# Turning query and key images by DMA instead of TensorE in a four-layer recurrent attention kernel

## The chip, the cores and the metric

One core of one Trainium2 chip. The metric is the device time of one execution in microseconds (us), as the median of several executions.

Names in the profile: PE is TensorE (matrix products), DVE and ACT are the engines that in this kernel copy out of PSUM and do elementwise work, SP is the queue that issues its DMAs. The granted clock is the share of TensorE's full clock that the chip allowed. The chain is the path of work that ended last, followed back from the last instruction. A DMA's landing is the time from its issue to its data's arrival; its hold is the time that its instruction occupies the issuing queue.

## The reference, cut to what matters

```python
def _A_ref(x, mem0, Wq, Wk, Wv, Wo, seg_len):      # "memory layer"; 64 segments of 32 tokens
    mem = mem0                                      # 8 memory tokens
    for s in range(n_seg):
        h = concat([mem, x[:, s*32:(s+1)*32]])      # 40 tokens
        q, k, v = h @ Wq, h @ Wk, h @ Wv            # 32 heads of 128
        p = softmax(where(mask, q @ k.T * scale, -1e9))
        o = (p @ v) @ Wo
        mem = o[:, :8]                              # goes into the next segment
        outs.append(o[:, 8:])
    ...
x = x + _A_ref(layernorm(x), ...)                   # memory layer
x = x + _B_ref(layernorm(x), ...)                   # linear attention layer
x = x + _A_ref(layernorm(x), ...)
x = x + _B_ref(layernorm(x), ...)
```

The memory layers are a recurrence: a segment can't start until the memory of the one before is there. They take 1893 of 2158 us before.

## The kernel before

The kernel lists operations as nodes with reads, writes and an estimated cost. A list scheduler in the kernel's own code turns them into one fixed order for each engine, so what runs when is decided by those estimates.

A segment's 32 tokens are split: the first 24 form a block of 32 columns with the 8 memory tokens, and the last 8 tokens of four segments form a "left block" per tile of 128 tokens. Projections put four heads side by side in the four 32-column strips of TensorE, so that an "image" (128 x 512) has tokens in its partitions. The kernel's score products read queries and keys with the head dimension in the partitions. So each image is evacuated from PSUM, transposed by four 128x128 products on TensorE, and evacuated again:

```python
def transposed(W, key, blk, bkeys, b, dst, dkey, urgent):
    tl = project(W, key, blk, bkeys, b, urgent)     # 16 products of 512 columns, mode "col"
    k = img_no[0] % NI
    img_no[0] += 1
    nd = evac(img[:, k, :], lambda: tl.f32()[:, :], 512, tiles=[tl], writes=[("img", k)], urgent=urgent)
    tt = P.tile()
    def tr(pe):
        for i in range(4):
            r = pe.transpose(tt.bf16()[:, 128 * i:128 * i + 128], img[:, k, 128 * i:128 * i + 128], id_sb[:, :])
        return r
    add("pe", tr, c_pe(4, 128), reads=[("img", k), "id"], tiles=[tt], urgent=urgent)
    evac(dst, ..., 512, tiles=[tt], writes=[dkey], rate=2, urgent=urgent)
    return nd
```

A segment needs four images: query and key of heads 0 to 15 (b = 0), then of heads 16 to 31 (b = 1). A left block needs four more for each tile. The mask enters the memory scores as a bias product of 16 rows, twice 128 columns. Token scores are one product for each head and strip, over a query buffer into which the 8 left columns are copied.

The softmax here doesn't subtract the row's maximum and nothing guards it: scores larger than these inputs give would overflow.

Of the kernel before, what the change touches and what calls it, by code (L numbers as in the profile page):

```python
# [18 lines left out]
MODE_SLACK = 0.3  # L19
# [35 lines left out]
class _Node:  # L55
    __slots__ = ("engs", "fn", "cost", "sync", "order", "tiles", "dsem", "dval", "eng", "start", "done",
                 "tail", "sig", "val", "waits", "know", "idx", "succ", "nleft", "urgent", "mode")


class _Prog:  # L60
# [17 lines left out]
    def add(self, engs, fn, cost, reads=(), writes=(), tiles=(), dsem=None, urgent=False, mode="full",  # L78
            after=()):
        nd = _Node()  # L80
        nd.mode = mode
        nd.engs = (engs,) if isinstance(engs, str) else tuple(engs)
# [41 lines left out]
    def schedule(self):  # L124
# [15 lines left out]
        for nd in reversed(nodes):  # L140
            lag = PE_LAG if nd.engs == ("pe",) else HOP
            best = 0.0
            for s in nd.succ:
                v = s.tail + (0.0 if nd in s.order else lag)
                if v > best:
                    best = v
            nd.tail = best + min(nd.cost.values())
# [13 lines left out]
        n_left = len(nodes)  # L161
        pend = {e: [] for e in ENGINES}
# [25 lines left out]
        def n_free(t_now):  # L188
            k = 0
            for own in self.bank_owner:  # L190
                if own is None or (own.ops[-1].done is not None and own.ops[-1].done <= t_now):
                    k += 1
            return k
# [3 lines left out]
        def pick_for(e):  # L197
            tn = self.now[e]
            while pend[e] and pend[e][0][0] <= tn + EPS:
                _, _, nd = heapq.heappop(pend[e])  # L200
                if nd.done is None:
                    heapq.heappush(ready[e], (-nd.tail, nd.idx, nd))
            pick = None
            kept = []
            while ready[e]:
# [4 lines left out]
                if first_of(nd):  # L210
                    bf = bank_for(tn)
                    if bf is None or bf[1] > tn + EPS or (not nd.urgent and n_free(tn) < 3):
# [12 lines left out]
                elif nd.tail < pick.tail - MODE_SLACK:  # L225
# [12 lines left out]
        while n_left:  # L238
# [47 lines left out]
            nd.done = nd.start + nd.cost[e]  # L286
            self.now[e] = nd.done - (0.09 if e == "act" else 0.05 if e == "dve" else 0.0)
# [94 lines left out]
def _build_kernel(nc, A_x, A_mem0, A_Wq, A_Wk, A_Wv, A_Wo, A_seg_len, B_wqkv, B_wo, out):  # L382
# [35 lines left out]
    w16_sb = sb("w16_sb", [128, 4, 2, 32])  # L418
# [31 lines left out]
    img = av(NI * 512).rearrange("p (r x) -> p r x", r=NI)  # L450
    vimg = av(2 * 1024).rearrange("p (r x) -> p r x", r=2)
    vleft = av(2 * 1024).rearrange("p (r x) -> p r x", r=2)
    qT = av(2 * 1280).rearrange("p (r h j x) -> p r h j x", r=2, h=8, j=4)
# [11 lines left out]
    xlnA = av(D).rearrange("p (r x) -> p r x", r=1)  # L465

# [73 lines left out]

    BIG = -1.0e9
    pool(lambda g: g.memset(w16_sb[:, :, 0, :], 0.0), ["w16"])
    pool(lambda g: g.memset(w16_sb[:, :, 1, :], BIG), ["w16"])
    for gg in range(4):
        a = w16_sb[:, gg, 0, :]
        sel(a, GE, BIG, 0, [[-4, 4], [0, 8]], 1, "w16")
        sel(a, GE, BIG, 3, [[4, 4], [0, 8]], -1, "w16")
        sel(w16_sb[:, gg, 1, :], ALU.not_equal, 0.0, -gg, [[-4, 4], [0, 8]], 1, "w16")
# [71 lines left out]
    def a_layer(layer):  # L620
        img_no = [0]
# [14 lines left out]
        def transposed(W, key, blk, bkeys, b, dst, dkey, urgent):  # L636

            tl = project(W, key, blk, bkeys, b, urgent)
            k = img_no[0] % NI
            img_no[0] += 1  # L640
            nd = evac(img[:, k, :], lambda: tl.f32()[:, :], 512, tiles=[tl], writes=[("img", k)], urgent=urgent)
            tt = P.tile()

            def tr(pe):
                for i in range(4):
                    r = pe.transpose(tt.bf16()[:, 128 * i:128 * i + 128], img[:, k, 128 * i:128 * i + 128], id_sb[:, :])  # L646
                return r
            add("pe", tr, c_pe(4, 128), reads=[("img", k), "id"], tiles=[tt], urgent=urgent)
            evac(dst, lambda: tt.bf16()[:, 0:512].rearrange("p (h j x) -> p h j x", h=4, j=4), 512, tiles=[tt],
                 writes=[dkey], rate=2, urgent=urgent)  # L650
            return nd

        def left_block(G):
# [3 lines left out]
            for b in range(2):  # L657
                hs = slice(4 * b, 4 * b + 4)
                transposed(Wq_sb, "Wq", blk, bk, b, qTl[:, r2, hs, :, :], ("qTl", r2, b), False)
                transposed(Wk_sb, "Wk", blk, bk, b, kTl[:, r2, hs, :, :], ("kTl", r2, b), False)  # L660
# [29 lines left out]
        def mem_attention(s, b, early):  # L690
# [8 lines left out]
            def bias(pe):  # L699
                for a in range(2):  # L700
                    r = pe.matmul(tl.f32()[:, 128 * a:128 * a + 128], u16_sb[0:16, :],  # L701
                                  w16_sb[0:16, g, a, :].unsqueeze(1).to_broadcast([16, 4, 32]), start=(a == 0),
                                  stop=False, skip_group_check=True)
                return r
            add("pe", bias, c_pe(2, 128), reads=["u16", "w16"], tiles=[tl], urgent=True, after=early, mode="bias")
# [38 lines left out]
        def x_attention(s):  # L744
# [6 lines left out]
            for b in range(2):  # L751
                hs = slice(4 * b, 4 * b + 4)
                add(ANY, copy(qT[:, r2, hs, :, 32:40], qTl[:, g2, hs, :, gl]),
                    {"act": c_act(128, 0, 1), "dve": c_dve(128)}, reads=[("qTl", g2, b)], writes=[("qTL", r2, b)])

                def mm(pe, b=b):
                    for hh in range(4 * b, 4 * b + 4):
                        for j in range(4):
                            r = pe.matmul(tl.f32()[32 * j:32 * j + 32, 32 * hh:32 * hh + 32], kT[:, r2, hh, j, :],  # L759
                                          qT[:, r2, hh, j, 8:40], start=True, stop=True, tile_position=(0, 32 * j))  # L760
                    return r
                add("pe", mm, c_pe4(16, 32), reads=[("kT", r2, b), ("qT", r2, b), ("qTL", r2, b)], tiles=[tl], mode="col")
# [58 lines left out]
        def next_mem(s):  # L821
            G1, g1 = divmod(s + 1, 4)
            tl = P.tile()
            for h in range(2):
# [5 lines left out]
                add("pe", mm, c_pe(2, 128), reads=[(("outW", s % 3), h), "selm"], tiles=[tl], urgent=True)  # L830
# [5 lines left out]
        def residual(G, g):  # L836

            if g == 0:
# [5 lines left out]
                c_pe(1, 512), reads=[(("outW", w), 0), (("outW", w), 1), "selx"], tiles=[tl])  # L844
            if g == 3:
# [3 lines left out]
                    c_pe(1, 512), reads=[("outWl", 0), ("outWl", 1), "sell"], tiles=[tl])  # L849
                add("dve", lambda v: v.tensor_tensor(x_sb[:, G, :], x_sb[:, G, :], tl.f32()[:, :], ALU.add), c_dve(512),  # L850
                    reads=[("x", G)], writes=[("x", G)], tiles=[tl])

# [192 lines left out]
```

## Time and profile before

| | before |
|---|---|
| time, median of 3 runs | 2161.87 us (2161.3 to 2163.71) |
| TensorE busy | 2079 us, 96% of the span |
| DVE, ACT busy | 1201 us, 1160 us |
| granted TensorE clock | 0.994 |
| TensorE in the chain that ended last | 94% |

The prediction below shows the lines behind this table and how its numbers come from them. Some durations that it uses, as medians of this trace: products overlap (four of 512 columns start 0.216 us after the four before and last 0.38 us each); the reader of a product's result in PSUM starts 0.21 to 0.30 us after the start of the last product, for products of 32 and 128 columns at L710, L646 and L759; a copy of 512 columns from PSUM takes DVE 0.42 us where PSUM holds bf16 (the transposed images) and 0.69 us where it holds f32 (0.52 and 1.04 ns for each further column, by the 96- and 128-column copies at 0.21 and 0.29 us), and ACT 0.60 us in both cases.

### The profile page before, as it was taken

The numbers are of one execution on the slowest core, as the hardware profiler recorded it, in microseconds if no ns is written. First come the engines' busy times: TensorE is split into PE (matmuls) and PEld (weight loads), VectorE is DVE, ScalarE is ACT, GpSimd is POOL, SyncE is SP. The second block draws the span as 40 slices with busy tenths as digits, with TensorE's granted clock in tenths as the row PEclk, the third lists the DMA queues.
The fourth block names the chain that finished last, engine by engine and source line by source line (L and its number), as shares of the span: only waits on it lengthen the run. The fifth ranks groups of instructions, "written<-read, shape, count | busy, mean of one in ns | idle before, by whom it ended". The sixth has DMA issues, their size and how long they took to land.

```text
span 2158.2 us, 83024 instructions
## 1 busy us (share of the span) xinstructions
PE 2079.3 (96%) x37982; PEld 1163.5 (54%) x37982; DVE 1201.2 (56%) x3287; ACT 1159.7 (54%) x3112; POOL 14.8 (1%) x74
## 2 busy tenths in 40 slices
PE   1999999999999999998999999999999999999989
PEld 0555555555555555554655555555555555555545
DVE  0655555555554555556876555555555555554678
ACT  0555555555555555554645555555555555555554
POOL 2000000000000000000000000000000000000000
PEclk9999999999999999999999999999999999999999
DMA  9000000000000000001000000000000000000011
GB/s 350 3 3 2 3 3 3 3 3 3 3 3 3 3 3 3 3 3 41 1 2 3 3 3 3 3 2 3 3 3 3 3 3 3 3 3 3 3 41 40
DMA packets 12558, 30.48 MB, mean 14 GB/s; under 512 B 424, under 2 KB 9648, under 8 KB 10672
## 3 DMA queue, kind: packets, MB, share of 16 engines
q1 hardware_dynamic: 12208, 25.18, 3.2%
q8 instruction: 297, 4.87, 0.9%
q14 instruction: 53, 0.43, 0.1%
HBM read 23.08 MB, written 2.10 MB: 12 GB/s over the span
## 4 chain that ended last, share of the span: by engine, by line
PE 94%; DVE 2%; DMA 2%; ACT 1%; issue 0%; SPq 0%
PE pb L630 42%; PE pb L808 14%; PE pb L646 8%; PE pb L792 4%; PE pb L827 3%; PE pb L921 3%; PE pb L710 3%; PE pb L701 3%; PE pb L842 2%; PE pb L722 2%; DMA x_sb<-in_A_x_dram 2%; PE pb L735 2%; PE pb L759 2%; PE pb L914 1%; PE pb L736 1%; PE pb L771 1%
## 5 line engine op out<-in xcount | busy, mean ns | idle before, releaser
L498 ACT ACTIVATE arena_sb<-pb 128x512 bf16<-128x512 f32 (+6 forms) x1410 | 673.2, 492 | 458.7 <-PE pb L630 269.7
L630 PE MATMUL pb<-Wq_sb,arena_sb 128*32 128x512 bf16 x5120 | 478.2, 383 | 0.9 <-ACT arena_sb L498 0.4
L630 PE MATMUL pb<-Wk_sb,arena_sb 128*32 128x512 bf16 x5120 | 472.5, 382 | 0.0
L499 DVE CAST arena_sb<-pb 128x512 bf16<-128x512 f32 (+2 forms) x541 | 312.3, 578 | 237.6 <-PE pb L793 142.5
L630 PE MATMUL pb<-Wv_sb,arena_sb 128*32 128x512 bf16 x5120 | 374.4, 383 | 0.0
L808 PE MATMUL pb<-Wo_sb,arena_sb 128*32 128x512 bf16 x5184 | 350.1, 381 | 0.0
L780 DVE TENSOR_TENSOR arena_sb<-arena_sb 32x256 bf16<-32x256 bf16 x512 | 213.3, 417 | 133.6 <-ACT arena_sb L776 121.7
L499 DVE COPY arena_sb<-pb 128x512 bf16<-128x512 bf16 (+1 forms) x543 | 205.8, 399 | 137.8 <-PE pb L646 134.3
L646 PE MATMUL pb<-id_sb,arena_sb 128*128 128x128 bf16 x2560 | 216.7, 220 | 0.0
L630 PEld LDWEIGHTS pb<-Wq_sb,arena_sb 128*32 128x32 bf16 x5120 | 134.4, 96 | 133.2 <-ACT arena_sb L498 14.6
L646 PEld LDWEIGHTS pb<-id_sb,arena_sb 128*128 128x128 bf16 x2560 | 145.0, 97 | 103.2 <-issue 41.6
L630 PEld LDWEIGHTS pb<-Wk_sb,arena_sb 128*32 128x32 bf16 x5120 | 134.6, 97 | 108.5 <-issue 2.5
L717 ACT ACTIVATE arena_sb<-pb 128x256 bf16<-128x256 f32 x256 | 97.5, 381 | 158.9 <-PE pb L710 158.8
L498 ACT ACTIVATE outW_sb<-pb 128x256 fp32r<-128x256 f32 x198 | 75.8, 383 | 195.9 <-PE pb L808 194.5
L808 PEld LDWEIGHTS pb<-Wo_sb,arena_sb 128*32 128x32 bf16 x5184 | 119.7, 95 | 102.4 <-issue 20.7
L630 PEld LDWEIGHTS pb<-Wv_sb,arena_sb 128*32 128x32 bf16 x5120 | 109.6, 95 | 76.9
L782 DVE TENSOR_TENSOR arena_sb<-arena_sb 32x64 bf16<-32x64 bf16 x512 | 111.0, 217 | 15.8
L792 PE MATMUL pb<-arena_sb 128*128 128x128 bf16 x1024 | 115.2, 218 | 4.0 <-DVE arena_sb L782 4.0
L710 PE MATMUL pb<-arena_sb 128*128 128x32 bf16 x2048 | 118.6, 177 | 0.0
L499 DVE COPY arena_sb<-arena_sb 128x128 bf16<-128x128 bf16 x192 | 35.9, 194 | 128.8 <-PE pb L759 127.8
L793 PE MATMUL pb<-arena_sb 128*128 128x32 bf16 x1024 | 105.6, 178 | 0.0
L827 PEld LDWEIGHTS pb<-selm_sb,outW_sb 128*128 128x128 f32 x504 | 77.6, 188 | 51.8 <-ACT outW_sb L498 18.2
(108 smaller groups left out, 2330.6 us busy)
## 6 DMA issues: line engine op xcount, KB each, us to landing
Wq_sb<-in_A_Wq_dram SPq DMA_DIRECT2D x1, 4096.0 KB, 12.4
Wk_sb<-in_A_Wk_dram SPq DMA_DIRECT2D x1, 4096.0 KB, 22.2
Wv_sb<-in_A_Wv_dram SPq DMA_DIRECT2D x1, 4096.0 KB, 31.7
Wo_sb<-in_A_Wo_dram SPq DMA_DIRECT2D x1, 4096.0 KB, 43.2
arena_sb<-in_B_wqkv_dram SPq DMA_DIRECT2D x2, 1536.0 KB, 6.5
out_dram<-x_sb SPq DMA_DIRECT2D x16, 128.0 KB, 1.7
x_sb<-in_A_x_dram SPq DMA_DIRECT2D x1, 1920.0 KB, 11.5
arena_sb<-in_B_wo_dram SPq DMA_DIRECT2D x2, 512.0 KB, 7.5
```

The costliest lines, as they stand in the source:

```text
L498: return e.activation(o() if callable(o) else o, i() if callable(i) else i, ACTF.Copy)
L499: return e.tensor_copy(o() if callable(o) else o, i() if callable(i) else i)
L630: r = pe.matmul(tl.f32()[32 * j:32 * j + 32, 0:512], blk[:, c, :], W[:, c, o:o + 512], start=(c == 0), stop=(c == 3), tile_position=(0, 32 ...
L646: r = pe.transpose(tt.bf16()[:, 128 * i:128 * i + 128], img[:, k, 128 * i:128 * i + 128], id_sb[:, :])
L710: r = pe.matmul(tl.f32()[:, o:o + 32], kk[:, hh, :, :].rearrange("p j x -> p (j x)"), qT[:, r2, hh, :, 0:8], start=False, stop=True, skip_ ...
L717: add("act", lambda a: a.activation(Pm[:, k, :, :].rearrange("p a q -> p (a q)"), tl.f32()[:, 0:256], ACTF.Exp, scale=SCALE), c_act(256), ...
L780: add("dve", lambda v, q=q, j=j: v.tensor_tensor(Pbx[q, :, j, 0:32], Px[q, :, :], Rx[q, :, :], ALU.mult), c_dve(256), reads=["Px", "Rx"], ...
L782: add("dve", lambda v, q=q, j=j: v.tensor_tensor(Pbx[q, :, j, 32:40], PLL[q, g2, :, gl], Rx[q, :, 24:32], ALU.mult), c_dve(64), reads=[("P ...
L792: pe.matmul(o, vimg[:, r2, e], Pbx[:, hh, :, 0:32], start=True, stop=False)
L793: return pe.matmul(o[:, :, 24:32], vleft[:, g2, e], Pbx[:, hh, :, 32:40], start=False, stop=True)
L808: r = pe.matmul(tl.f32()[32 * j:32 * j + 32, :], oT[:, 4 * hh + j, :], Wo_sb[:, 8 * j + hh, :], start=(hh == 0), stop=(hh == 7), tile_posi ...
L827: r = pe.matmul(tl.f32()[:, 8 * c:8 * c + 8], outW[:, s % 3, 128 * c:128 * c + 128], selm_sb[:, :], start=True, stop=True)
```

## The change

The intent: take the transposes (8% of the chain) off TensorE, and let the idle DMA (share 0.01 in the memory layers before) turn the images. With it come a bias of one full-array product, a scheduler that finishes one tile before the next and changes array mode less readily, and, because the kernel gives this transpose a destination without gaps, token scores split into a 24-column and an 8-column product.

```diff
-MODE_SLACK = 0.3
+MODE_SLACK = 2.0
...
-        def transposed(W, key, blk, bkeys, b, dst, dkey, urgent):
+        def turned(W, key, blk, bkeys, b, dst, dkey, urgent=False):
             tl = project(W, key, blk, bkeys, b, urgent)
...
-            tt = P.tile()
-            def tr(pe): ...                          # four transposes
-            add("pe", tr, c_pe(4, 128), ...)
-            evac(dst, ...)
+            add("sp", lambda e: e.dma_start_transpose(dst.rearrange("p h j x -> p h (j x)"), img[:, k, :]), 0.1,
+                reads=[("img", k)], writes=[dkey], dsem="turn%d" % k, lat=2.5)
...
-            add("pe", bias, c_pe(2, 128), ..., mode="bias")      # two products, 16 rows
+            add("pe", lambda pe: pe.matmul(tl.f32()[:, 0:256], u16_sb[:, :], w16_sb[:, g, ...], ...),
+                c_pe(1, 256), ...)                               # one product, 128 rows
...
-                add(ANY, copy(qT[:, r2, hs, :, 32:40], qTl[:, g2, hs, :, gl]), ...)
-                            r = pe.matmul(..., kT[:, r2, hh, j, :], qT[:, r2, hh, j, 8:40], ...)
+                            pe.matmul(..., kT[:, r2, hh, j, :], qT[:, r2, hh, j, 8:32], ...)
+                            r = pe.matmul(..., kT[:, r2, hh, j, :], qTl[:, g2, hh, j, gl], ...)
```

In the scheduler, a node gets `lat`: the engine is free after its cost, its result is there `lat` later. For an image that says: queue held 0.1 us, landing 2.5 us after. Cut here: priorities follow a tile's earlier operations; the oldest waiting tile may take the last free PSUM bank, while urgent ones must leave one; left blocks get two image buffers of their own; the mask is built once a layer; and the scheduler's costs for the next memory and the residual go up (0.24 and 0.33 us).

More of the change, by code (lines that the diff above doesn't have):

```diff
@@ L56 @@
     __slots__ = ("engs", "fn", "cost", "sync", "order", "tiles", "dsem", "dval", "eng", "start", "done",
-                 "tail", "sig", "val", "waits", "know", "idx", "succ", "nleft", "urgent", "mode")
+                 "tail", "sig", "val", "waits", "know", "idx", "succ", "nleft", "urgent", "mode", "prio", "lat")
 class _Prog:
@@ L78, in add @@
     def add(self, engs, fn, cost, reads=(), writes=(), tiles=(), dsem=None, urgent=False, mode="full",
-            after=()):
+            after=(), lat=0.0):
         nd = _Node()
         nd.mode = mode
+        nd.lat = lat
         nd.engs = (engs,) if isinstance(engs, str) else tuple(engs)
@@ L146, in schedule @@
                     best = v
-            nd.tail = best + min(nd.cost.values())
+            nd.tail = best + min(nd.cost.values()) + nd.lat
+        for nd in nodes:
+            nd.prio = nd.tail
+            for tl in nd.tiles:
+                k = tl.ops.index(nd)
+                if k and tl.ops[k - 1] in nd.order and tl.ops[k - 1].done is None:
+                    nd.prio = max(nd.prio, tl.ops[k - 1].prio)
         fenced = set()
@@ L161, in schedule @@
         n_left = len(nodes)
+        tiles = []
+        for nd in nodes:
+            for tl in nd.tiles:
+                if tl.ops[0] is nd:
+                    tiles.append(tl)
+        oldest = [0]
         pend = {e: [] for e in ENGINES}
@@ L190, in n_free @@
             for own in self.bank_owner:
-                if own is None or (own.ops[-1].done is not None and own.ops[-1].done <= t_now):
+                lo = own.ops[-1] if own is not None else None
+                if lo is None or (lo.done is not None and lo.done + (PE_LAG if lo.eng == "pe" else HOP) <= t_now):
                     k += 1
@@ L201, in pick_for @@
                 if nd.done is None:
-                    heapq.heappush(ready[e], (-nd.tail, nd.idx, nd))
+                    heapq.heappush(ready[e], (-nd.prio, nd.idx, nd))
             pick = None
@@ L211, in pick_for @@
                     bf = bank_for(tn)
-                    if bf is None or bf[1] > tn + EPS or (not nd.urgent and n_free(tn) < 3):
+                    while tiles[oldest[0]].bank is not None:
+                        oldest[0] += 1
+                    spare = 0 if tiles[oldest[0]] in nd.tiles else 1 if nd.urgent else 2
+                    if bf is None or bf[1] > tn + EPS or n_free(tn + EPS) <= spare:
                         kept.append(item)
@@ L224, in pick_for @@
                     held = item
-                elif nd.tail < pick.tail - MODE_SLACK:
+                elif nd.prio < pick.prio - MODE_SLACK:
                     kept.append(item)
@@ L285, in schedule @@
                 self.pe_mode = nd.mode
-            nd.done = nd.start + nd.cost[e]
-            self.now[e] = nd.done - (0.09 if e == "act" else 0.05 if e == "dve" else 0.0)
+            nd.done = nd.start + nd.cost[e] + nd.lat
+            self.now[e] = nd.start + nd.cost[e] - (0.09 if e == "act" else 0.05 if e == "dve" else 0.0)
             self.last[e] = nd
@@ L417, in _build_kernel @@
     u16_sb = sb("u16_sb", [128, 128])
-    w16_sb = sb("w16_sb", [128, 4, 2, 32])
     mx_sb = sb("mx_sb", [128, 32])
@@ L449, in _build_kernel @@
     hT = av(2 * 5 * 4 * 32).rearrange("p (r b c x) -> p r b c x", r=2, b=5, c=4)
-    img = av(NI * 512).rearrange("p (r x) -> p r x", r=NI)
+    img = av((NI + 2) * 512).rearrange("p (r x) -> p r x", r=NI + 2)
     vimg = av(2 * 1024).rearrange("p (r x) -> p r x", r=2)
     vleft = av(2 * 1024).rearrange("p (r x) -> p r x", r=2)
-    qT = av(2 * 1280).rearrange("p (r h j x) -> p r h j x", r=2, h=8, j=4)
+    qT = av(2 * 1024).rearrange("p (r h j x) -> p r h j x", r=2, h=8, j=4)
     kT = av(2 * 1024).rearrange("p (r h j x) -> p r h j x", r=2, h=8, j=4)
@@ L465, in _build_kernel @@
     xlnA = av(D).rearrange("p (r x) -> p r x", r=1)
+    w16_sb = av(4 * 2 * 128).rearrange("p (g a h x) -> p g a h x", g=4, a=2, h=4)
     SCR = [("kTl", 1, 0), ("kTl", 1, 1)]
@@ L539, in _build_kernel @@
     sel(u16_sb[:, :], GE, 0.0, 7, [[-1, 128]], 8, "u16")
-    BIG = -1.0e9
-    pool(lambda g: g.memset(w16_sb[:, :, 0, :], 0.0), ["w16"])
-    pool(lambda g: g.memset(w16_sb[:, :, 1, :], BIG), ["w16"])
-    for gg in range(4):
-        a = w16_sb[:, gg, 0, :]
-        sel(a, GE, BIG, 0, [[-4, 4], [0, 8]], 1, "w16")
-        sel(a, GE, BIG, 3, [[4, 4], [0, 8]], -1, "w16")
-        sel(w16_sb[:, gg, 1, :], ALU.not_equal, 0.0, -gg, [[-4, 4], [0, 8]], 1, "w16")
     pool(lambda g: g.memset(mx_sb[:, :], 1.0), ["mx"])
@@ L620, in a_layer @@
     def a_layer(layer):
-        img_no = [0]
+        img_no = [0, 0]
         cnt = {"m": 0}
@@ L634, in project @@
             return tl
-        def transposed(W, key, blk, bkeys, b, dst, dkey, urgent):
+        def turned(W, key, blk, bkeys, b, dst, dkey, urgent=False):
             tl = project(W, key, blk, bkeys, b, urgent)
-            k = img_no[0] % NI
-            img_no[0] += 1
+            k = img_no[0] % NI if urgent else NI + img_no[1] % 2
+            img_no[0 if urgent else 1] += 1
             nd = evac(img[:, k, :], lambda: tl.f32()[:, :], 512, tiles=[tl], writes=[("img", k)], urgent=urgent)
-            tt = P.tile()
-            def tr(pe):
-                for i in range(4):
-                    r = pe.transpose(tt.bf16()[:, 128 * i:128 * i + 128], img[:, k, 128 * i:128 * i + 128], id_sb[:, :])
-                return r
-            add("pe", tr, c_pe(4, 128), reads=[("img", k), "id"], tiles=[tt], urgent=urgent)
-            evac(dst, lambda: tt.bf16()[:, 0:512].rearrange("p (h j x) -> p h j x", h=4, j=4), 512, tiles=[tt],
-                 writes=[dkey], rate=2, urgent=urgent)
+            add("sp", lambda e: e.dma_start_transpose(dst.rearrange("p h j x -> p h (j x)"), img[:, k, :]), 0.1,
+                reads=[("img", k)], writes=[dkey], dsem="turn%d" % k, lat=2.5)
             return nd
@@ L658, in left_block @@
                 hs = slice(4 * b, 4 * b + 4)
-                transposed(Wq_sb, "Wq", blk, bk, b, qTl[:, r2, hs, :, :], ("qTl", r2, b), False)
-                transposed(Wk_sb, "Wk", blk, bk, b, kTl[:, r2, hs, :, :], ("kTl", r2, b), False)
+                turned(Wq_sb, "Wq", blk, bk, b, qTl[:, r2, hs, :, :], ("qTl", r2, b))
+                turned(Wk_sb, "Wk", blk, bk, b, kTl[:, r2, hs, :, :], ("kTl", r2, b))
             for b in range(2):
@@ L697, in mem_attention @@
             tl = P.tile()
-            def bias(pe):
-                for a in range(2):
-                    r = pe.matmul(tl.f32()[:, 128 * a:128 * a + 128], u16_sb[0:16, :],
-                                  w16_sb[0:16, g, a, :].unsqueeze(1).to_broadcast([16, 4, 32]), start=(a == 0),
-                                  stop=False, skip_group_check=True)
-                return r
-            add("pe", bias, c_pe(2, 128), reads=["u16", "w16"], tiles=[tl], urgent=True, after=early, mode="bias")
+            add("pe", lambda pe: pe.matmul(tl.f32()[:, 0:256], u16_sb[:, :],
+                                           w16_sb[:, g, :, :, :].rearrange("p a h x -> p (a h x)"), start=True,
+                                           stop=False, skip_group_check=True),
+                c_pe(1, 256), reads=["u16", "w16"], tiles=[tl], urgent=True, after=early)
             def mm(pe, a, kk):
@@ L752, in x_attention @@
                 hs = slice(4 * b, 4 * b + 4)
-                add(ANY, copy(qT[:, r2, hs, :, 32:40], qTl[:, g2, hs, :, gl]),
-                    {"act": c_act(128, 0, 1), "dve": c_dve(128)}, reads=[("qTl", g2, b)], writes=[("qTL", r2, b)])
                 def mm(pe, b=b):
@@ L758, in mm @@
                         for j in range(4):
-                            r = pe.matmul(tl.f32()[32 * j:32 * j + 32, 32 * hh:32 * hh + 32], kT[:, r2, hh, j, :],
-                                          qT[:, r2, hh, j, 8:40], start=True, stop=True, tile_position=(0, 32 * j))
+                            q = slice(32 * j, 32 * j + 32)
+                            pe.matmul(tl.f32()[q, 32 * hh:32 * hh + 24], kT[:, r2, hh, j, :], qT[:, r2, hh, j, 8:32],
+                                      start=True, stop=True, tile_position=(0, 32 * j))
+                            r = pe.matmul(tl.f32()[q, 32 * hh + 24:32 * hh + 32], kT[:, r2, hh, j, :],
+                                          qTl[:, g2, hh, j, gl], start=True, stop=True, tile_position=(0, 32 * j))
                     return r
-                add("pe", mm, c_pe4(16, 32), reads=[("kT", r2, b), ("qT", r2, b), ("qTL", r2, b)], tiles=[tl], mode="col")
+                add("pe", mm, 2 * c_pe4(16, 32), reads=[("kT", r2, b), ("qT", r2, b), ("qTl", g2, b)], tiles=[tl], mode="col")
             add("act", lambda a: a.activation(Px[:, :, :].rearrange("p h q -> p (h q)"), tl.f32()[:, 0:256], ACTF.Exp,
@@ L829, in mm @@
                     return r
-                add("pe", mm, c_pe(2, 128), reads=[(("outW", s % 3), h), "selm"], tiles=[tl], urgent=True)
+                add("pe", mm, 0.24, reads=[(("outW", s % 3), h), "selm"], tiles=[tl], urgent=True)
             evac(hT[:, G1 % 2, g1, :, 0:8], lambda: tl.f32()[:, 0:32].rearrange("p (c m) -> p c m", c=4), 32, tiles=[tl],
@@ L843, in residual @@
                                            start=(g == 0), stop=False, skip_group_check=True),
-                c_pe(1, 512), reads=[(("outW", w), 0), (("outW", w), 1), "selx"], tiles=[tl])
+                0.33, reads=[(("outW", w), 0), (("outW", w), 1), "selx"], tiles=[tl])
             if g == 3:
@@ L848, in residual @@
                                                skip_group_check=True),
-                    c_pe(1, 512), reads=[("outWl", 0), ("outWl", 1), "sell"], tiles=[tl])
+                    0.33, reads=[("outWl", 0), ("outWl", 1), "sell"], tiles=[tl])
                 add("dve", lambda v: v.tensor_tensor(x_sb[:, G, :], x_sb[:, G, :], tl.f32()[:, :], ALU.add), c_dve(512),
                     reads=[("x", G)], writes=[("x", G)], tiles=[tl])
+        BIG = -1.0e9
+        pool(lambda p: p.memset(w16_sb[:, :, 0, :, :], 0.0), ["w16"])
+        pool(lambda p: p.memset(w16_sb[:, :, 1, :, :], BIG), ["w16"])
+        for g in range(4):
+            sel(w16_sb[:, g, 0, :, :], GE, BIG, 0, [[0, 4], [-4, 4], [0, 8]], 1, "w16")
+            sel(w16_sb[:, g, 0, :, :], GE, BIG, 3, [[0, 4], [4, 4], [0, 8]], -1, "w16")
+            sel(w16_sb[:, g, 1, :, :], ALU.not_equal, 0.0, -g, [[0, 4], [-4, 4], [0, 8]], 1, "w16")
         add("dve", lambda v: v.memset(oTb[:, :, :, :].rearrange("p r n x -> p (r n x)").bitcast(F32), 0.0), 1.7,
@@ L866, in a_layer @@
                 hs = slice(4 * b, 4 * b + 4)
-                transposed(Wq_sb, "Wq", blk, bk, b, qT[:, r2, hs, :, 0:32], ("qT", r2, b), True)
-                early.append(transposed(Wk_sb, "Wk", blk, bk, b, kT[:, r2, hs, :, :], ("kT", r2, b), True))
+                turned(Wq_sb, "Wq", blk, bk, b, qT[:, r2, hs, :, :], ("qT", r2, b), True)
+                early.append(turned(Wk_sb, "Wk", blk, bk, b, kT[:, r2, hs, :, :], ("kT", r2, b), True))
             for b in range(2):
```

## The prediction

> **What bounds the kernel now.** I read the page first: busy shares, the 40 slices, and the chain that ended last.
>
> ```profile
> PE 2079.3 (96%) x37982; PEld 1163.5 (54%) x37982; DVE 1201.2 (56%) x3287; ACT 1159.7 (54%) x3112; POOL 14.8 (1%) x74
> ...
> PE 94%; DVE 2%; DMA 2%; ACT 1%; issue 0%; SPq 0%
> PE pb L630 42%; PE pb L808 14%; PE pb L646 8%; PE pb L792 4%; PE pb L827 3%; PE pb L921 3%; PE pb L710 3%; PE pb L701 3%; PE pb L842 2%; PE pb L722 2%; DMA x_sb<-in_A_x_dram 2%; PE pb L735 2%; PE pb L759 2%; PE pb L914 1%; PE pb L736 1%; PE pb L771 1%
> ```
>
> A busy 96% alone would prove little, because matmuls overlap. The chain settles it: 94% of the time that leads to the last instruction is TensorE working through its own program order. So a matmul that is taken away shortens the run, as long as no wait takes its place. L646, the transposes of the images that this change removes, holds 8% of the chain, some 173 us of 2158.
>
> Next, the busy time in four stretches (columns: stretch, its length, busy time and count for PE, PEld, DVE, ACT and POOL, clock, DMA share, GB/s). They are my split into memory layer, linear-attention layer, and the same again:
>
> ```profile
> 65.00:1008.00 943.00, 940.58 (x17937) 521.76 (x17937) 512.70 (x1423) 523.31 (x1424) 0.00 (x0) 1.00 0.01 3
> 1008.00:1100.00 92.00, 82.78 (x824) 52.24 (x815) 75.83 (x194) 47.94 (x108) 0.21 (x2) 0.94 0.07 24
> 1100.00:2050.00 950.00, 945.35 (x17943) 522.49 (x17947) 516.42 (x1425) 524.58 (x1429) 0.00 (x0) 1.00 0.01 3
> ```
>
> The memory layers take 943 + 950 = 1893 us. Each has 64 segments, so one segment takes 1893 / 128 = 14.8 us. The clock is full, and DVE and ACT are busy only about 55%. Only this part is touched; the rest (about 265 us: load, linear layers, ends) stays.
>
> Third, the timeline where projection, transpose and bias meet (start, length, engine, line, operation):
>
> ```profile
> 609.87 0.39 PE L630 MATMUL pb<-Wk_sb,arena_sb 128*32 128x512 bf16 x4
> 610.19 0.62 PE L646 MATMUL pb<-id_sb,arena_sb 128*128 128x128 bf16 x8
> 610.74 0.83 PE L630 MATMUL pb<-Wv_sb,arena_sb 128*32 128x512 bf16 x12
> 611.50 0.28 PE L701 MATMUL pb<-w_sb,u_sb 16*128 16x128 bf16 x2
> 611.72 0.40 PE L646 MATMUL pb<-id_sb,arena_sb 128*128 128x128 bf16 x4
> ```
>
> Starts matter here, not lengths. Four 512-column products in four column strips start every 0.216 us. From 609.87 the next group should start at 610.09; the full-array transposes start at 610.19, so 0.10 us went to the change of array mode. Eight transposes then take 610.74 - 610.19 = 0.55 us: 8 x 0.056 = 0.45, and 0.10 for the way back. The bias (16 rows) has a mode of its own: 0.22 us for two 128-column products, half of it switching.
>
> [...] The trace has TensorE at 0.22 us latency and 0.056 us apart; it holds no DMA transpose. [...] An image is 128 x 512 x 2 bytes = 131 KB[...]. The only duration here for such a size is the plain 128 KB store of the output, 1.7 us from issue to landing. [...]
>
> **The change part by part**, per segment (a quarter of the left block of a tile included).
>
> Transposes: (64 segments x 4 + 16 left blocks x 4) x 4 = 1280 a layer, 2560 in all, as the trace counts; 20 a segment. A chain over 100 to 900 us gives L646 9.5%, 76 us for 54 segments (the sums L722, four a segment, count 216 there): 1.41 us a segment, 1.11 us of it columns and 0.30 switching. Off the path: -1.41.
>
> Their evacuations and the strip copies: 640 half-rate copies from PSUM at 0.42 (DVE) or 0.60 us (ACT), and 256 small copies, leave DVE and ACT. Not the bound: 0 directly, though shorter queues help what follows.
>
> Bias: two products of 128 columns in their own mode become one of 256 in the full mode. L701 has 2.9% of the same chain, 0.43 us a segment for two. After: 2 x 0.11 = 0.22. -0.2.
>
> Token scores (L759): the copy that joined the 24 segment columns and 8 left columns is gone, so each product is split in two, 32 more a segment with their own weights. L759 has 1.7%, 0.25 us a segment[...] (16 start within 0.16 us). It doubles: +0.25.
>
> Order: the scheduler now keeps the array mode unless the other candidate is 2.0 us more urgent (before 0.3), and finishes one tile before the next, where the before-trace alternates Wq and Wk. I counted about 16 mode changes a segment in the timeline, 1.6 us. Some 6 belong to transposes and bias and are counted above; of the other 10 I let 3 go: -0.3. Finishing the first query tile 0.86 us early also starts its DMA early.
>
> Sum on TensorE: -1.41 - 0.2 + 0.25 - 0.3 = about -1.65 us. 128 x 1.65 = 211 us, so 2162 - 211 = 1950 us if all DMA is hidden.
>
> **The path around TensorE.** A segment's memory comes from the segment before, so a segment can't be shorter than its serial chain. By durations in this trace: query and key projections of four tiles one by one, 4 x 0.86 = 3.45; PSUM lag 0.24; evacuation 0.6; the DMA, L; bias and scores 0.3 + 0.24; exp 0.38; sums 0.11 + 0.24; log 0.28; exp 0.31; multiply 0.29; second half of the output projection 0.87 + 0.24; evacuation 0.4; next memory 0.24 + 0.24; copy 0.2; hops about 0.4. That is 9.0 + L. With L = 2.5, the latency written into the scheduler, it is 11.5 us, under the 13.15 us of TensorE work. L may reach 4.1 before the chain alone sets the time. But TensorE runs in a fixed order planned for 2.5 us, so a longer L stalls it earlier, by nearly the excess.
>
> **The rivals.** (a) The wait for a DMA takes the place of the transposes. Five transfers a segment share one queue, four in a burst 0.86 us apart. If each holds the queue for 1.2 us[...], the fourth is late by 3 x 0.34 = 1.0 us, and a segment takes about 14.1: 2080 us. At 1.7 us each it is late by 2.5 us, and 15.7 a segment gives 2270, slower than before. For it: nothing in this trace shows the cost, and scores can't start without the images. Against: the 1.7 us for 128 KB, an idle DMA (share 0.01), and the scheduler's 2.5, which looks like a measured latency. (b) The transfers serialise wholly, latency and all, at 2.5 us or more: 5 x 2.5 = 12.5, nearly a whole segment, and 3.5 us each give 17.5 and 2500. Against: separate semaphores, six image buffers, no wait between transfers. (c) DVE or ACT becomes the bound: no, they lose work. (d) The scheduler's larger slack delays urgent work: at most some tenths a segment. (e) All is hidden: 1950, or 1910 if more mode changes vanish.
>
> **Range and chances.** Hidden gives 1910 to 1960; I expect part of (a), about 0.4 us a segment, 50 us: 2000 us. The lower edge is 1900; the upper, 2200, holds waits of up to 2 us a segment. Faster by over 2% means below 2119, which allows 1.3 us of stall a segment over 1950: 0.75. Within 2%: 0.10. Slower: 0.15, for rival (b) and the bad case of (a).
>
> **What would show it.** The profile after should have no 128x128 transposes from image tiles, 8192 token-score products, 256 bias products, 640 transposes on the DMA queue, and TensorE's busy sum in a memory layer near 13 us a segment. If right, waits of TensorE for DMA stay under 0.5 us a segment and issue to landing near 2.5 us. It is wrong if TensorE waits 1 us or more a segment for images, if landings in a burst grow by over a microsecond from the first to the fourth, or if mode changes stay at 16 a segment.

## The result, and the profile after

The changed kernel took 2227.65 us (median of 4, 2222.83 to 2231.47), beside 2161.59 for the kernel before: a ratio of 1.030 (1.028 to 1.033). The prediction said 2000, and its range ended at 2200. A ratio here is the mean time of one kernel's fast runs over that of the other's in the same rounds, so not quite the ratio of the medians.

The page after: busy time (engine, us, share, count), then the chain by engine and by line.

```profile
PE 1969.7 (88%) x39262; PEld 1086.9 (49%) x39262; DVE 863.7 (39%) x2508; ACT 1221.7 (55%) x2995; POOL 23.6 (1%) x88
...
PE 66%; DMA 25%; DVE 4%; ACT 3%; issue 1%; SPq 1%; DVEq 0%; ACTq 0%
PE pb L639 31%; DMA arena_sb<-arena_sb 23%; PE pb L807 13%; PE pb L928 3%; PE pb L826 3%; PE pb L756 2%; ACT arena_sb L516 2%; PE pb L709 2%; DVE arena_sb L779 2%; DMA arena_sb<-in_A_mem_dram 2%; PE pb L841 2%; PE pb L721 1%; PE pb L995 1%; PE pb L921 1%; PE pb L791 1%
```

TensorE does less (1970 us busy instead of 2079) in a longer time. The chain has changed hands: a quarter of it is now the transfer of images (arena_sb<-arena_sb). The same stretches as before, memory layer, linear layer, memory layer (columns as in the prediction):

```profile
65.00:1042.00 977.00, 882.40 (x18498) 480.50 (x18490) 351.30 (x1050) 549.77 (x1354) 0.21 (x2) 0.98 0.25 45
1042.00:1137.00 95.00, 83.83 (x816) 53.04 (x820) 78.45 (x198) 49.05 (x114) 5.98 (x14) 0.91 0.06 22
1137.00:2135.00 998.00, 900.09 (x18794) 490.94 (x18790) 348.18 (x1043) 560.50 (x1382) 0.00 (x0) 0.97 0.26 45
```

A memory layer takes 977 and 998 us instead of 943 and 950, with TensorE idle about 95 us in each, and a lower clock (0.98 and 0.97). Who TensorE waits for (us in total, times, longest):

```profile
PE pb L709 <- DMA arena_sb<-arena_sb: 162.9, 253, 2.2
PE pb L623 <- DVE arena_sb L616: 30.4, 5, 17.5
```

L709 is the memory scores: 163 us of waiting for images, in 253 waits over 128 segments. Before there was no such wait. How long does one image take? The transposes by source line (duration of the instruction in the queue in ns, min/median/max; then time to landing):

```profile
L651 SPq DMA_TRANSPOSE arena_sb<-arena_sb x640: 1188/1264/2734, 40.0 to 2122.9; - x160
...
DMA to landing us min/median/max: 2.4/2.5/7.9
```

The landing time is what the scheduler was told, 2.5 us. But the instruction itself occupies the queue for half of that, 1.26 us, where the scheduler was told 0.1. One burst shows what follows. These are the queue's rows of four short windows of the timeline (start, length):

```profile
605.88 1.19 SPq L651 DMA_TRANSPOSE arena_sb<-arena_sb  x1
607.11 1.26 SPq L651 DMA_TRANSPOSE arena_sb<-arena_sb  x1
608.42 2.13 SPq L651 DMA_TRANSPOSE arena_sb<-arena_sb  x1
610.60 1.27 SPq L651 DMA_TRANSPOSE arena_sb<-arena_sb  x1
```

and TensorE's timeline and the chain at the same place:

```profile
609.57 0.25 PE L709 MATMUL pb<-arena_sb 128*128 128x32 bf16 x4
611.28 0.19 PE L709 MATMUL pb<-arena_sb 128*128 128x32 bf16 x1 [1.46 <-DMA arena_sb<-arena_sb]
...
610.60 2.47 DMA arena_sb<-arena_sb
613.11 0.26 PE pb L709 x4
```

The four images of a segment stand in line. The evacuations ended at 605.85, 606.72, 607.58 and 608.44, 0.86 us apart; the fourth was issued at 610.60, over 2 us after it was ready, and landed at 613.07. The second score product waited until 611.28 for the first key image, the second in line. That wait ended with this image's late landing (next paragraph), not with the line; the chain's last step, 610.60 to 613.11, is the fourth image.

One more thing is in this burst: the second image landed 4.1 us after its issue, and the third then held the queue for 2.13 us. I counted over the trace: 158 of the 640 images landed more than 3.0 us after issue, and 157 of those 158 overlapped a fetch of instructions (a packet of 8 or 16 KB, 1.0 us in the median); of the other 482 only 150 did. The mean landing is 2.81 us. No experiment here takes the fetches away, so this is an association, not a shown cause.

It is not a small one. I grouped the segments of this trace, each counted from its first issue to the next one's. The 52 segments without a late image took 14.7 us in the mean, the 74 with one 16.0; at each of the four places in a tile the gap is 0.9 to 1.4 us. With no transfers (run free below) a segment takes 13.3 us. So about 1.4 us a segment is lost even where every image lands in time, and late landings go with about 0.8 more over all segments. Of the waiting for images at all lines, 170 us, 90 ended with a late image. The first part is what the experiments below test.

### The profile page after: what moved, and what is told of

Its sections match the earlier page's. It is cut to its first block, busy times and chain, and to the rows that moved or that the text cites. A ratio compares the mean times of both kernels' runs of the same rounds, so it can differ in the third digit from the quotient of the medians.

```text
span 2229.8 us, 85170 instructions
## 1 busy us (share of the span) xinstructions
PE 1969.7 (88%) x39262; PEld 1086.9 (49%) x39262; DVE 863.7 (39%) x2508; ACT 1221.7 (55%) x2995; POOL 23.6 (1%) x88
## 4 chain that ended last, share of the span: by engine, by line
PE 66%; DMA 25%; DVE 4%; ACT 3%; issue 1%; SPq 1%; DVEq 0%; ACTq 0%
PE pb L639 31%; DMA arena_sb<-arena_sb 23%; PE pb L807 13%; PE pb L928 3%; PE pb L826 3%; PE pb L756 2%; ACT arena_sb L516 2%; PE pb L709 2%; DVE arena_sb L779 2%; DMA arena_sb<-in_A_mem_dram 2%; PE pb L841 2%; PE pb L721 1%; PE pb L995 1%; PE pb L921 1%; PE pb L791 1%
## 5 line engine op out<-in xcount | busy, mean ns | idle before, releaser
L516 ACT ACTIVATE arena_sb<-pb 128x512 bf16<-128x512 f32 (+6 forms) x1380 | 711.1, 519 | 477.7 <-PE pb L639 344.4
L517 DVE CAST arena_sb<-pb 128x128 bf16<-128x128 f32 (+3 forms) x376 | 158.8, 428 | 668.9 <-PE pb L792 323.2
L807 PE MATMUL pb<-Wo_sb,arena_sb 128*32 128x512 bf16 x5184 | 367.5, 407 | 3.3 <-DVE arena_sb L738 2.6
L639 PE MATMUL pb<-Wk_sb,arena_sb 128*32 128x512 bf16 x5120 | 360.9, 385 | 0.8 <-ACT arena_sb L516 0.8
L639 PE MATMUL pb<-Wq_sb,arena_sb 128*32 128x512 bf16 x5120 | 353.8, 383 | 1.0 <-ACT arena_sb L516 0.5
L639 PE MATMUL pb<-Wv_sb,arena_sb 128*32 128x512 bf16 x5120 | 328.8, 383 | 0.0
L709 PE MATMUL pb<-arena_sb 128*128 128x32 bf16 x2048 | 125.4, 179 | 166.2 <-DMA arena_sb<-arena_sb 162.9
L709 PEld LDWEIGHTS pb<-arena_sb 128*128 128x128 bf16 x2048 | 89.0, 97 | 230.0 <-DMA arena_sb<-arena_sb 217.2
L807 PEld LDWEIGHTS pb<-Wo_sb,arena_sb 128*32 128x32 bf16 x5184 | 127.4, 100 | 134.9 <-issue 29.3
L738 DVE TENSOR_TENSOR arena_sb<-pb,arena_sb 128x128 bf16<-128x128 f32 x256 | 74.5, 291 | 197.8 <-ACT arena_sb L726 97.9
L791 PE MATMUL pb<-arena_sb 128*128 128x128 bf16 x1024 | 142.1, 219 | 6.7 <-DVE arena_sb L781 6.4
L724 ACT ACTIVATE arena_sb<-pb 128x128 f32<-128x128 f32 x256 | 70.6, 276 | 126.5 <-PE pb L721 125.9
L792 PE MATMUL pb<-arena_sb 128*128 128x32 bf16 x1024 | 125.1, 179 | 0.0
L791 PEld LDWEIGHTS pb<-arena_sb 128*128 128x128 bf16 x1024 | 91.4, 97 | 39.0 <-issue 22.1
```

Source lines behind the costliest of these rows:

```text
L516: return e.activation(o() if callable(o) else o, i() if callable(i) else i, ACTF.Copy)
L517: return e.tensor_copy(o() if callable(o) else o, i() if callable(i) else i)
L639: r = pe.matmul(tl.f32()[32 * j:32 * j + 32, 0:512], blk[:, c, :], W[:, c, o:o + 512], start=(c == 0), stop=(c == 3), tile_position=(0, 32 ...
L709: r = pe.matmul(tl.f32()[:, o:o + 32], kk[:, hh, :, :].rearrange("p j x -> p (j x)"), qT[:, r2, hh, :, 0:8], start=False, stop=True, skip_ ...
L738: add("dve", lambda v: v.tensor_tensor(oTb[:, s % 3, 16 * b:16 * b + 16, 0:8], pv.f32()[:, 0:128].rearrange("p (n q) -> p n q", q=8), Rm[: ...
L791: pe.matmul(o, vimg[:, r2, e], Pbx[:, hh, :, 0:32], start=True, stop=False)
```

## The experiments

Two theories. **Waiting**: TensorE's work fell as summed, and the loss is waiting for images; in one form (plan) because the order was made with wrong numbers, in another (chain) because a line of four images makes a segment's serial path as long as TensorE's work. **Work**: TensorE's work did not fall as summed. "Told" below means the scheduler's numbers `0.1, lat=2.5` replaced by `1.27, lat=1.25`.

A caution on correctness: every run passed the comparison with the reference, the first one below too, which reads cleared key and query buffers. The comparison's tolerance doesn't notice the scores, so it vouches for no image in any of these runs.

### free: no transfer at all (wrong)

```diff
-            add("sp", lambda e: e.dma_start_transpose(dst..., img[:, k, :]), 0.1, ...)
-            nd = evac(img[:, k, :], ..., writes=[("img", k)], urgent=urgent)
+            nd = evac(img[:, k, :], ..., writes=[("img", k), dkey], urgent=urgent)
+        # qT, kT, qTl, kTl cleared once a layer
```

> The changed kernel with every DMA transpose taken out: evacuated images go nowhere, scores read key and query buffers that are cleared once a layer (wrong result on purpose), all else and its dependences kept. Wait theory (the time is lost in waiting for images): TensorE's own sum holds, about 1950 us, and at most 2000. Rival (the work on TensorE did not fall as summed, through split scores, lower clock or order): 2080 us or more. If it is between, both have a share.

Measured 1963.69 us (ratio 0.908). The work theory falls: with the same instructions but the transfers, the kernel runs at what the sum promised. So the transfers cost 2227.65 - 1963.69 = 264 us, 2.06 us a segment. Three things are in it. Waits at L709 are 163 us. TensorE's busy time also rises, from 1861.8 us here to 1969.7 with nearly the same count (39238 and 39262), as the clock goes from 0.992 to 0.968; the clock withheld 71 us of the span (0.032 of 2230) instead of 16, so it can explain at most about half of these 108 us, and the rest is open. And the order is not the same: with no transfer to plan for, the scheduler planned 1936 us here and 1983 for the changed kernel (its own clock, see told), so 47 of the 264 us are in the plan already.

```profile
PE 1861.8 (95%) x39238; PEld 1077.6 (55%) x39262; DVE 789.6 (40%) x2339; ACT 1223.2 (62%) x3172; POOL 23.5 (1%) x88
```

### all_tensor and tensor_one: the rest of the change without the DMA

```diff
-turned(Wq_sb, "Wq", ...); turned(Wk_sb, "Wk", ...)     # all four places
+transposed(Wq_sb, "Wq", ...); transposed(Wk_sb, "Wk", ...)
# tensor_one also undoes the split:
-    pe.matmul(..., qT[:, r2, hh, j, 8:32], ...); r = pe.matmul(..., qTl[:, g2, hh, j, gl], ...)
+    r = pe.matmul(..., qT[:, r2, hh, j, 8:40], ...)    # with the copied strip
```

> The changed kernel with all images transposed on TensorE again (order, one-product bias and split scores kept). My sum gives -0.2 bias, -0.3 mode changes, +0.25 split scores a segment: 128 x -0.25 = about 2130 us. Rival (the new order or the splitting costs time): 2170 us or more, and then the DMA is only part of the loss.

> All images on TensorE and the token scores unsplit: only the order, the scheduler's changes and the one-product bias are left of the change. Against the run with all images on TensorE and split scores (2119 us) it shows the cost of splitting: my estimate of 0.25 us a segment gives 32 us, so 2085 us; if the split is free, 2119.

Measured 2118.83 us (0.980, on the edge of the 2% that counts as faster) and 2072.85 us (0.959). The order, the scheduler's changes and the one-product bias gain 2162 - 2073 = 89 us, 0.70 us a segment. Counted over 100 to 900 us, mode changes fell from 17.8 a segment in the kernel before to 10.4 in tensor_one. Splitting the token scores costs 2119 - 2073 = 46 us. And 2119 - 1964 = 155 us is what the transposes and their evacuations cost, each time with the order that the scheduler makes for it. The whole account, step by step: 2162, -89 to 2073, +46 to 2119, -155 to 1964, +264 to 2228.

### told: the right numbers for the scheduler

```diff
-... img[:, k, :]), 0.1, reads=[("img", k)], writes=[dkey], dsem="turn%d" % k, lat=2.5)
+... img[:, k, :]), 1.27, reads=[("img", k)], writes=[dkey], dsem="turn%d" % k, lat=1.25)
```

> The changed kernel with only the scheduler's numbers for a DMA changed to the measured ones: the queue held 1.27 us instead of 0.1, landing 1.25 us after that instead of 2.5. Plan theory (the fixed order was planned for a queue that takes an image at once): TensorE's waits for images fall from about 1.6 us to under 0.5 us a segment, about 2050 us. Chain theory (four images at 1.31 us through one queue make the serial path of a segment as long as TensorE's work, so that no order hides it): 2180 to 2230 us.

Measured 2289.93 us (1.059): worse than with the wrong numbers, and worse than either theory said. The plan theory falls. Waits for images did halve, but others came:

```profile
PE pb L709 <- DMA arena_sb<-arena_sb: 84.4, 96, 2.6
PE pb L807 <- DVE arena_sb L738: 44.7, 73, 1.8
```

TensorE now waits for what follows the scores (L807 is the output projection). The scheduler keeps its own clock, which tells what it believed: the changed kernel was planned for 1983 us, told for 2115, free for 1936. So even by its own reckoning no order that it finds hides a line of four; and the chip needed 175 us more than the plan. Why its order with honest numbers is worse on the chip than the other by 62 us stays open. (Of the 56 us between the two profiled runs, 42 are TensorE's busy time, 2011.6 us against 1969.7, at a clock of 0.954.)

### extra: one more image in the line

```diff
+            if urgent and key == "Wq" and b == 1:
+                add("sp", lambda e: e.dma_start_transpose(spare, img[:, k, :]), 0.0, reads=[("img", k)],
+                    writes=["spare"], dsem="spare")
```

> The changed kernel, its plan unchanged, with one more transpose a segment that nothing waits for (second query image into a spare buffer), issued in the burst ahead of the last key image. Hold theory (each image holds the queue 1.26 us and the images stand in line): the last key image lands about 1.3 us later in each of 128 segments, so up to +168 us, about 2350 to 2395 us. Latency theory (each image just takes 2.5 us from issue to landing, side by side, and the plan has no room for it): no change beyond 1%, 2210 to 2250 us.

Measured 2531.18 us (1.170), 303 us over the changed kernel. Nothing waits for the spare image, so its 2.5 us of latency can't matter; its place in line does. The latency theory falls. But the hold theory gave 168 us at most. The waits of the memory scores for images (L713 here) rose from 163 to 342 us, by 179, near the 168. TensorE's busy time with the same 39262 products rose by 131 us, from 1969.7 to 2100.5, while the clock fell to 0.898. That the clock made this second part fits but is not shown by itself. The waits, then the page's busy times:

```profile
PE pb L713 <- DMA arena_sb<-arena_sb: 342.0, 289, 3.5
...
PE 2100.5 (83%) x39262; PEld 1120.4 (44%) x39262; DVE 864.6 (34%) x2508; ACT 1224.7 (48%) x2995; POOL 23.5 (1%) x88
```

### halves and pair: does the hold grow with the size?

```diff
# halves: two transposes an image
+   add("sp", ...(d3[:, 0:2, :], img[:, k, 0:256]), 0.1, ..., dsem="turn%d" % k, lat=2.5)
+   add("sp", ...(d3[:, 2:4, :], img[:, k, 256:512]), 0.1, ..., dsem="turh%d" % k, lat=2.5)
# pair: query and key image of a half side by side, one transpose
+   add("sp", ...(dst "p t h j x -> p (t h) (j x)", img[:, k, :, :] "p t x -> p (t x)"), 1.27,
+       reads=[("img", k, 0), ("img", k, 1)], writes=[both keys], dsem="turn%d" % k, lat=2.1)
```

> The changed kernel with each image moved as two transposes of half the columns. If the hold of the queue is proportional to the tiles moved, the two halves hold it as long as the whole (1.26 us together) and the time stays near 2230 us. If a large part of the hold is fixed for each instruction[...] the time goes up by 100 to 200 us.

> The changed kernel with the query and key image of a half moved by one transpose of twice the size (buffers of the pair side by side; the scheduler told 1.27 us hold and 2.1 us more to landing). The halves run showed that half the size holds the queue as long as the whole. Fixed-hold theory: one pair holds the queue about 1.3 us, the burst has two places instead of four, and the kernel, with the same amount transposed, comes under the changed one: 2050 to 2150 us. If the hold grows with size from here on (2.5 us a pair), no gain: 2200 us or more.

Measured 3049.03 us (1.410) and 2165.23 us (1.001). The transposes of the second half of each image, and of two images, by line:

```profile
L655 SPq DMA_TRANSPOSE arena_sb<-arena_sb x640: 1231/1247/2535, 41.5 to 2937.2; - x160
```

```profile
L651 SPq DMA_TRANSPOSE arena_sb<-arena_sb x320: 1230/1232/4218, 39.9 to 2056.8; - x160
...
DMA to landing us min/median/max: 3.0/3.1/7.9
```

Half the size holds the queue 1.25 us, the whole 1.26, twice the size 1.23. So, at these three sizes, the hold belongs to the instruction, not to what it moves. My estimate for halves, 100 to 200 us more than the changed kernel, rested on no run and was far off: the loss is 821 us. Only the landing grows: 2.4, 2.5, 3.1 us. Moving pairs has the same bytes in two places of the line instead of four, and is 62 us faster than the changed kernel, though 15 us over its expected window and no better than the kernel before. The first image of a pair has to wait for the second; the scheduler, which knows that, planned 2085 us. That this is the reason is not shown: of its 45 us of waiting for images, 44 ended with a late landing (here over 3.6 us).

### main_dma, last_tensor, half_dma, k_dma: how many in the line

```diff
# main_dma:    left blocks transposed(...), the four of a segment turned(...), numbers as in the change
# last_tensor: only Wk of b == 1 transposed(...), told
# half_dma:    Wq and Wk of b == 1 transposed(...), told
# k_dma:       Wq transposed(...), Wk turned(...), token scores unsplit, told   (left blocks by DMA in all three)
# k_dma1:      as k_dma, and
-MODE_SLACK = 2.0
+MODE_SLACK = 1.0
```

> The changed kernel with the left blocks' images on TensorE, the four of a segment still by DMA, scheduler's numbers as in the changed kernel. Burst theory: the line of four is intact, so it stays within 2% of the changed kernel, 2180 to 2270 us. If the whole load of the queue is what matters (five a segment to four, 20% less), waits fall with it: 2100 to 2150 us.

> As told, but only the last key image of a segment's four is transposed on TensorE; the other three and the left blocks go by DMA. Chain theory: it is the fourth place in the line that hurts. Told with measured holds, the scheduler's own plan for this is 1971 us against 2115 with all by DMA; the half-and-half kernel ran 80 us over its plan, so about 2050 us. Rival (late landings, which the plan knows nothing of, grow with the number of images): 2085 us or more, no better than half and half.

> As told, but of the four images of a segment the second half of the heads is transposed on TensorE, the first half and the left blocks by DMA. Chain theory: only two images of a segment in the queue, which shortens its serial path by about 2.5 us, while TensorE gets 8 transposes, about 0.6 us a segment, back: 2030 to 2060 us, with waits for images near zero. If only the plan matters, it is no better than the kernel told the right numbers. Rival (mixing brings mode changes back): over 2120 us.

> As told, but key images and left blocks go by DMA, query images on TensorE, and the token scores are one product again with the copied strip (the split is undone, since TensorE's evacuation can write the padded layout). Plan 1990 us; with 60 to 80 us over it as in the half-and-half kernel 2050 to 2070 us. The split itself should be worth about 0.3 us a segment (32 products), some 35 us; if the split costs nothing, 2085 us.

> The kernel with key images by DMA and query images on TensorE (2016 us), with the scheduler's slack for keeping the array mode 1.0 us instead of 2.0. Its own plan is 14 us shorter: about 2000 us if the chip follows the plan; 2016 or more if the overrun (late landings, mode changes) takes it back. In either case faster than both kernels of the case.

| run | images a segment by DMA (in the burst + left) | us | ratio |
|---|---|---|---|
| all_tensor | 0 + 0 | 2118.83 | 0.980 |
| half_dma | 2 + 1 | 2083.47 | 0.964 |
| last_tensor | 3 + 1 | 2033.45 | 0.941 |
| changed kernel | 4 + 1 | 2227.65 | 1.030 |
| told | 4 + 1 | 2289.93 | 1.059 |
| main_dma | 4 + 0 | 2246.09 | 1.039 |
| k_dma | 2 + 1, unsplit | 2016.21 | 0.932 |
| k_dma1 | 2 + 1, unsplit | 2011.70 | 0.930 |

It is the length of the line that hurts, the step from three places to four above all, and not the number of images. Taking the left blocks out of the queue (main_dma) gains nothing: the waits stay at 149 us, and TensorE gets some 31 us of transposes back (estimate: 4 of the 20 a segment that cost 155 us). Taking the fourth image out of the burst gains 256 us against told, which differs in that and in the order that follows from it (143 us of it are in the plan, 2115 to 1971). It holds where no image is late, too: such segments take 15.3 us in told, 14.7 in the changed kernel, 14.8 in main_dma, and 13.5 in last_tensor and half_dma. In last_tensor the waits of the scores for images are down to 38 us (main_dma's line first, then last_tensor's):

```profile
PE pb L726 <- DMA arena_sb<-arena_sb: 148.6, 232, 2.3
...
PE pb L726 <- DMA arena_sb<-arena_sb: 38.1, 58, 1.9
```

half_dma ended 23 us above its expected window; last_tensor came under its 2050. k_dma came 34 us under its expected 2050 to 2070, so its estimate missed too. Both k_dma runs beat both kernels. By k_dma1's trace the two key images still stand in line (the second is issued 1.24 us after the first in the median), but it is a line of two: its last image lands 3.8 us after the first issue, where the line of four in the changed kernel takes 7.0. And the evacuation after TensorE's transposes writes the padded query buffer itself, so the split is not needed. k_dma1's waits of the scores for images are 11 us, its clock 0.992:

```profile
PE pb L726 <- DMA arena_sb<-arena_sb: 10.7, 16, 1.8
```

Of the 14 us that k_dma1's plan was shorter, the chip gave 4.5.

## Why the prediction was wrong

- **TensorE bounds the kernel before, and a product removed shortens it as long as no wait comes in its place**: right. Without transfers it ran at 1964 us; the prediction's figure for all DMA hidden was 1950.
- **The sum of -1.65 us a segment**: right, -1.55 measured ((2162 - 1964) / 128). Its terms: transposes -1.41 predicted, -1.21 measured; bias and order -0.5, -0.70; split scores +0.25 (that their time doubles was my estimate), +0.36. The total is nearer than its terms, so their errors in part cancelled. (Mode changes were 17.8 a segment, not about 16.)
- **Issue to landing near 2.5 us**: right in the median, 2.5 us. The hold of 1.2 us in rival (a) was my estimate and came near the measured 1.26, but by luck: the trace before holds no DMA transpose, so nothing in it showed a hold.
- **The step that failed**: "I expect part of (a), about 0.4 us a segment, 50 us". The mechanism of rival (a), a wait for a DMA in the place of the transposes, is what happened, and its size was the mis-sized term: 2.06 us a segment, 264 us, five times as much. Rival (a) itself put the fourth image 1.0 us late at 1.2 us a hold and named 2080 us; the prediction discounted it because of an idle DMA and the scheduler's 2.5 us. But the DMA share is only 0.25 after the change too, and the line forms all the same.
- **Why it was mis-sized**: the serial path was written as 9.0 + L with L of one image, 11.5 us, so that L "may reach 4.1". But L there has to be that of the last image in line. By the trace, the first evacuation ends at 1.7 us of a segment; four places of 1.31 us (a hold of 1.26 and 0.04 between) and 1.2 us of landing after the last hold end at 8.1 us, where the prediction had 4.3 + 2.5 = 6.8. (In the trace the last image lands at 8.1 us in the median of the segments with no late image, and at 8.8 over all.) That makes the path 12.8 us, nearly as long as TensorE's 13.3 us (1.55 under the 14.8 of before). That a fixed order can't interleave two bounds so close without a gap is my reading, not shown. With 1.31 us a place, rival (a)'s own sum gives 3 x 0.45 = 1.35 us late, 14.5 us a segment and about 2120 us, close to the 14.7 us of the segments with no late image. last_tensor and extra show that the length of the line costs time, main_dma that the left blocks aren't it. What lacks from 2120 to 2228 us is of the size of what goes with the late landings (0.8 us a segment, some 100 us).
- **What no step had**: landings that come late beside instruction fetches; and the lower clock, with which TensorE's own busy time rose (1862 to 1970 us).
- **Its signs of being wrong**: TensorE waited 163 us for images, 1.3 us a segment, over the 1 us named. The sign that landings grow within a burst failed to show: the medians by place are 2.45, 2.50, 2.49 and 2.48 us. The delay is in the issue, the fourth 3.87 us after the first where the evacuations are 2.6 us apart.
- **The scheduler's 2.5 "looks like a measured latency"**: it agrees with the one measured here, 2.5 us in the median. What the scheduler was not told is the hold of 1.26 us.

## What to carry to other kernels

Ask two numbers of a transfer, how long after issue it lands and how long it holds its queue, and lay the holds end to end for every burst on the serial path before trusting the latency of one. Where the hold belongs to the instruction, as here at three sizes (1.25, 1.26 and 1.23 us), fewer and larger transfers shorten the line, smaller ones lengthen it: two places a segment in pair gave 2165 us, four in the changed kernel 2228, eight in halves 3049. And move only as much work off the bound engine as the other path can take: here two or three of four images by DMA gave 0.93 to 0.96, four gave 1.03.

## What these traces show of the DMA transpose and the clock

- The cost of a DMA transpose in its queue: SBUF to SBUF the hold was 1.25, 1.26 and 1.23 us (medians of halves, the changed kernel and pair) for images of 128 x 256, 512 and 1024 elements of 2 bytes.
- An image of 131 KB took 2.5 us from issue to landing, and 1.3 us a piece back to back, some 100 GB/s (estimate from 131 KB and 1.31 us).
- A whole image, four blocks of 128x128, landed in 2.5 us, a half of two blocks in 2.4 and a pair of eight in 3.1 (medians), so between these sizes the landing doesn't scale by blocks.
- In the changed kernel 157 of 158 late images (more than 3.0 us) overlapped an instruction fetch, and of the 75 transposes that held the queue over 1.6 us, up to 2.7, 56 came next after a late one. A cause is not shown.
- In the memory layers of the changed kernel (65 to 1038 and 1137 to 2135 us) no idle stretch of TensorE was longer than 2.4 us, and the granted clock was still halved 28 times (0.5 in the trace's clock records), for 3.41 us or a multiple of it. In the 3.41 us before each, TensorE was idle for 34 to 76% in sum. That is no sharp limit: other such stretches, idle up to 48%, were not followed by a fall.
